# A planned attention-and-MLP kernel: first chunks loaded in parts, weight bits shifted in SBUF, two engines for low parts, another order of work

## The chip, the cores and the metric

The kernel runs on one core of a Trainium2 chip. The metric is the device time of an execution in microseconds (us), and three of them were taken. The engines are called PE (TensorE), PEld (its weight loads), DVE (VectorE), ACT (ScalarE), POOL (GpSimd) and SP (SyncE, which issues most loads here).

## What is computed

B is 4, H 8 heads of D = 64, S = 768 tokens, the model width 512. A decaying state per head gives y, and y goes through a gated layer: a causal convolution of five taps makes the gate, `w_val` and `w_out` are two 512x512 products.

```python
for t in range(S):
    state = gamma * state + einsum('bhd,bhe->bhde', k[:, :, t], v[:, :, t])
    y[:, :, t] = scale * einsum('bhd,bhde->bhe', q[:, :, t], state)
x = y.transpose(0, 2, 1, 3).reshape(B, S, H * D)
gate = 1 / (1 + exp(-causal_conv(x, conv_w)))     # 5 taps per channel
return (gate * (x @ w_val)) @ w_out
```

## The kernel before

The tokens are cut into 6 chunks of 128, times 4 batches: 24 groups, in the order chunk by chunk. `load` brings one group as a 1 MB tile `att` of four parts: q and k by dimension (parts 0 and 1), v and k by token (parts 2 and 3). Four such tiles exist (`LB`).

**Attention.** The four groups of chunk 0 go by `first_scores` (matmuls into the one score tile `sy`, L363), `first_mask` (DVE multiplies `sy` by a table, L396), `first_y` (matmuls into the one tile `ye`, L441) and `evac` (DVE copies `ye` times a decay into `x`, L504). `first_state` (L408) adds k times v to the state `z_ps`, after `decay` (POOL, L339) has scaled k. From group 4 on, `head` and then a `visit` and `rest_of_visit` per group do scores, state and y in one block of small matmuls (L424, L408, L424, L350), with `mask` (L372), `snap`, `turn` and `evac` on DVE and ACT.

**MLP.** Products run in three passes for accuracy: each operand is split into a high part (rounded by ACT) and a low part (value minus high part): `round_x` and `rest_x` for x (L514, L519), `round_gv` and `rest_gv` for the gated values (L632, L636), `cv_round` and `cv_low` for the weights (L577, L581). `val` (L610) makes a tile of 12 matmuls for each chunk and 128 channels, `outp` (L644) one for each chunk and batch: 48 tiles in all, called V and O below. `tap` (ACT L593 once, DVE L595 four times per tile) and `sigmoid` (ACT L602) make the gate, `gated` (DVE L625) multiplies it by the V tile in PSUM and so frees one of two banks `mm`. So a third V tile cannot start before `gated` has read the first.

**Weights.** The 8 weight tiles (w0 to w3 of `w_val`, w4 to w7 of `w_out`) arrive as 64-bit numbers in 512 KB pieces `wst`. Each is turned into fp32 by `cv_scale` (ACT, into a PSUM tile `acc`, L544), `cv_bits` (DVE shift and mask in `acc`, L548), `cv_top` (DVE, the sign from `wst`, the rest from `acc`, into `top`, L554), `cv_up` (ACT, L563) and `cv_sum` (POOL, L567); then `cv_round` on ACT and `cv_low` on POOL split it. The two `acc` tiles are those of the convolution.

**Order.** `plan` (L80 on) takes every step with a due time, an engine, a cost from the table `TIMES` and what it reads and writes, and writes out one order for all engines; a step with `other` may go to a second engine (no step has one before). `WORK` is the string of what PE does: s, y, z, p (first scores, y, state, table), h (head), v (visit), w (load a weight), V, O. `LOADS` is the order of the first loads on SP's queue. Where the plan sees PE idle at the start, it puts `filler` matmuls into `ye` (L672).

Of the kernel before, what the change touches and what calls it, by code (L numbers as in the profile page):

```python
# [21 lines left out]
LB = 4  # L22
# [230 lines left out]
def tile_retention_gated_mlp(  # L253
# [50 lines left out]
    masks = [  # L304
        mlp.tile([P, 512], F32, name="o_sb")[:, 0:384].rearrange("p (j k t) -> p j k t", j=2, t=HALF)
        for x in range(2)
    ]
# [71 lines left out]
    def first_table(x, part):  # L379


        vd = vd_sb[:, 0, 4 * x:4 * x + 4].rearrange("p (j s) -> p j s", s=2)
        if part == 0:
            nc.vector.tensor_tensor(
                masks[x][:, :, 0:3:2],
                vd.unsqueeze(3).broadcast_to([P, 2, 2, HALF]),
                tri_sb.unsqueeze(1).unsqueeze(1).broadcast_to([P, 2, 2, HALF]),
                op=ALU.mult,
            )
        else:  # L390
            nc.scalar.copy(masks[x][:, :, 1], vd[:, :, 0].unsqueeze(2).broadcast_to([P, 2, HALF]))

    def first_mask(g, x):
        if x == 0:
            us[g] = mlp.tile([P, 768], F32, name="u", bufs=2).rearrange("p (x j k t) -> p x j k t", x=2, j=2, t=HALF)
        nc.vector.tensor_tensor(  # L396
            us[g][:, x],
            sy[:, x, 0:384].rearrange("p (j k t) -> p j k t", j=2, t=HALF),
            masks[x],
            op=ALU.mult,  # L400
        )
# [133 lines left out]
    def cv_scale(n):  # L535


        size = high(n).shape[1]
# [5 lines left out]
        nc.scalar.mul(cvt[n][0].bitcast(F32), high(n).bitcast(F32), 2.0 ** -112)  # L544

    def cv_bits(n):
        bits = cvt[n][0]
        nc.vector.tensor_scalar(  # L548
            bits, bits, 3, 0x7FFFFFFF, op0=ALU.logical_shift_left, op1=ALU.bitwise_and
        )  # L550
# [25 lines left out]
    def cv_round(n):  # L576
        nc.scalar.copy(parts_of(n)[0], cvt[n][1].bitcast(F32))  # L577

    def cv_low(n):
# [1 line left out]
        nc.gpsimd.tensor_tensor(l, cvt[n][1].bitcast(F32), h.bitcast(F32), op=ALU.subtract)  # L581
# [282 lines left out]
    for p, (kind, n) in enumerate(LOADS):  # L864
# [3 lines left out]
        elif kind == "a":  # L868
            load_at(t, n)
        elif kind == "q":  # L870
            at(t, "DMA", 0.4, [], [("att", 0, "qk")], load, 0, slice(0, 2)).mb = 0.5
        elif kind == "v":
            at(t, "DMA", 0.4, [], [("att", 0, "vk"), ("att", 0, "kn")], load, 0, slice(2, 4)).mb = 0.5
# [142 lines left out]
```

## Time and profile before

| what | value |
|---|---|
| median of 3 runs | 214.03 us (213.93 to 215.69) |
| the profiled execution, its own time | 213.34 us |
| its span in the trace | 211.5 us |
| PE, DVE, ACT, POOL busy | 202.0, 125.3, 109.7, 106.0 us |
| granted PE clock | 0.999 |
| bytes read and written | 29.46 and 6.29 MB |

Busy time of PE also counts the fillers and the overlap of pipelined matmuls. A row of a timeline reads: start, length, engine, line, operation, tile written <- tiles read, shape, count, and in brackets the idle time before it with what ended it. In the trace each fp32 matmul of the attention is two records, so a block of 16 in the code is x32.

### The profile page before, as it was taken

Reading aid. Unit: us, or ns where it says so; the run is one execution under the profiler, and the core shown is the slowest. Engines: PE = TensorE matmul, PEld = TensorE weight load, DVE = VectorE, ACT = ScalarE, POOL = GpSimd, SP = SyncE. Lnnn points to the kernel's source line nnn. Section 1 sums busy time; section 2 is a strip of 40 time slices with the busy share of each in tenths; the row PEclk is TensorE's granted clock in tenths of the full one; section 3 lists DMA queues with packets and bytes.
Section 4 is the critical chain, followed back from the end, with each engine's and each line's share of the span. In section 5 each row is a group of like instructions: output and inputs, shape, how many; then the busy total and the mean of one; then the engine's idle time right before and its main releaser. Section 6 shows DMA issues by size and latency. Waiting matters only on the chain.

```text
span 211.5 us, 7837 instructions
## 1 busy us (share of the span) xinstructions
PE 202.0 (96%) x3500; PEld 160.1 (76%) x3500; DVE 125.3 (59%) x193; ACT 109.7 (52%) x237; POOL 106.0 (50%) x93
## 2 busy tenths in 40 slices
PE   8976799999999999999999999999999999999993
PEld 3655578876787887888888887877777788888883
DVE  0467799994889322799589813499505599211000
ACT  2377657974793533964686334455345445311321
POOL 0279987899953773538565336242044624202200
PEclk9999999999999999999999999999999999999999
DMA  6999995647656703866352715521110010121122
GB/s 196 395 418 412 417 373 198 228 181 229 270 203 198 277 29 110 293 234 268 124 225 108 262 38 206 181 116 50 53 53 3 3 50 0 51 100 51 50 101 99
DMA packets 8677, 36.24 MB, mean 171 GB/s; under 512 B 1090, under 2 KB 1474, under 8 KB 5700
## 3 DMA queue, kind: packets, MB, share of 16 engines
q1 hardware_dynamic: 4896, 29.43, 37.5%
q10 hardware_dynamic: 3748, 6.32, 7.9%
q8 instruction: 27, 0.44, 0.9%
q14 instruction: 6, 0.05, 0.1%
HBM read 29.46 MB, written 6.29 MB: 169 GB/s over the span
## 4 chain that ended last, share of the span: by engine, by line
PE 79%; POOL 6%; ACT 2%; DVE 2%; issue 1%; DMA 1%; ACTq 0%; DVEq 0%
PE mm L610 31%; PE mm L644 29%; PE sy L424 9%; PE sy L350 4%; PE z_ps L408 3%; POOL wol L581 2%; POOL top L567 2%; POOL gvl L636 1%; PE ye L672 1%; DMA out_dram<-o_sb 1%; DVE u L396 1%; DVE x L504 1%; PE ye L441 0%; ACT o_sb L654 0%; PE sy L363 0%
## 5 line engine op out<-in xcount | busy, mean ns | idle before, releaser
L595 DVE SCALAR_TENSOR_TENSOR acc<-x,cw_sb,acc 128x512 f32<-128x512 f32 x96 | 68.1, 752 | 4.6 <-ACT acc L593 3.4
L636 POOL TENSOR_TENSOR gvl<-gate,gvh 128x512 fp32r<-128x512 f32 x24 | 30.9, 1288 | 45.0 <-ACT gvh L632 42.2
L519 POOL TENSOR_TENSOR xl<-x,xh 128x512 fp32r<-128x512 f32 x24 | 30.8, 1286 | 31.2 <-ACT xh L514 29.6
L644 PE MATMUL mm<-wol,gvh 128*128 128x512 f32 (+1 forms) x100 | 37.8, 390 | 0.5 <-POOL wol L581 0.5
L644 PE MATMUL mm<-woh,gvh 128*128 128x512 f32 (+1 forms) x100 | 37.6, 390 | 0.0
L644 PE MATMUL mm<-woh,gvl 128*128 128x512 f32 (+1 forms) x100 | 37.5, 389 | 0.0
L610 PE MATMUL mm<-xh,wvh 128*128 128x512 f32 x96 | 35.3, 399 | 0.0
L610 PE MATMUL mm<-xl,wvh 128*128 128x512 f32 x96 | 33.9, 406 | 0.0
L339 POOL TENSOR_TENSOR att<-att,small_sb 128x512 f32<-128x512 f32 x24 | 25.1, 1048 | 12.0 <-DMA small_sb<-in_small_dram 6.8
L372 DVE TENSOR_TENSOR u<-sy,small_sb 128x512 f32<-128x512 f32 x20 | 13.8, 688 | 24.9 <-PE sy L350 20.8
L625 DVE TENSOR_TENSOR gate<-mm,gate 128x512 f32<-128x512 f32 x24 | 16.4, 685 | 20.0 <-PE mm L610 20.0
L610 PE MATMUL mm<-xh,wvl 128*128 128x512 f32 x96 | 26.6, 397 | 0.0
L654 ACT COPY o_sb<-mm 128x512 f32<-128x512 f32 (+1 forms) x25 | 14.3, 571 | 23.0 <-PE mm L644 22.1
L632 ACT CAST gvh<-gate 128x512 fp32r<-128x512 f32 x24 | 14.8, 617 | 18.8 <-DVE gate L625 18.0
L644 PEld LDWEIGHTS mm<-wol,gvh 128*128 128x128 f32 x100 | 18.7, 188 | 5.3 <-POOL wol L581 1.4
L644 PEld LDWEIGHTS mm<-woh,gvh 128*128 128x128 f32 x100 | 18.7, 188 | 4.5 <-ACT woh L577 0.3
L644 PEld LDWEIGHTS mm<-woh,gvl 128*128 128x128 f32 x100 | 18.7, 188 | 4.1
L602 ACT ACTIVATE gate<-acc 128x512 f32<-128x512 f32 x24 | 14.4, 602 | 14.2 <-DVE acc L595 8.4
L610 PEld LDWEIGHTS mm<-xh,wvh 128*128 128x128 f32 x96 | 17.8, 188 | 4.4 <-ACT xh L514 0.2
L610 PEld LDWEIGHTS mm<-xh,wvl 128*128 128x128 f32 x96 | 17.9, 188 | 4.2
L610 PEld LDWEIGHTS mm<-xl,wvh 128*128 128x128 f32 x96 | 17.7, 188 | 4.4
L514 ACT CAST xh<-x 128x512 fp32r<-128x512 f32 x24 | 14.9, 620 | 9.5 <-DVE x L504 9.3
(49 smaller groups left out, 249.4 us busy)
## 6 DMA issues: line engine op xcount, KB each, us to landing
att<-in_att_dram SPq DMA_DIRECT2D x23, 1024.0 KB, 5.1
out_dram<-o_sb ACTq DMA_DIRECT2D x23, 256.0 KB, 2.1
wst<-in_w_dram SPq DMA_DIRECT2D x8, 512.0 KB, 10.2
att<-in_att_dram SPq DMA_DIRECT2D x2, 512.0 KB, 4.5
out_dram<-o_sb ACTq DMA_DIRECT2D x2, 128.0 KB, 1.7
small_sb<-in_small_dram SPq DMA_DIRECT2D x1, 68.0 KB, 5.4
cw_raw<-in_conv_w_dram ACTq DMA_DIRECT2D x1, 20.0 KB, 5.3
u<-in_pos_dram ACTq DMA_DIRECT2D x1, 5.0 KB
```

What stands on the lines that cost most here:

```text
L339: nc.gpsimd.tensor_tensor(v, v, vd_sb[:, c, :].unsqueeze(2).broadcast_to([P, 8, HALF]), op=ALU.mult)
L424: nc.tensor.matmul(sy[cols, h, off:off + HALF], lhsT=lhsT, rhs=rhs, start=start, stop=True, skip_group_check=True,)
L514: nc.scalar.copy(xh[n][:, :, b], xs[n][:, :, b, HALO:])
L519: nc.gpsimd.tensor_tensor(xl[n][:, :, b], xs[n][:, :, b, HALO:], xh[n][:, :, b].bitcast(F32), op=ALU.subtract)
L595: nc.vector.scalar_tensor_tensor(acc, x[:, :, k:k + P], cw_sb[:, m, k:k + 1], acc, op0=ALU.mult, op1=ALU.add,)
L602: nc.scalar.activation(gate[n, m], accs.pop((n, m)), AF.Sigmoid)
L610: nc.tensor.matmul(vps[n, m], lhsT=w[:, m, ct * P:(ct + 1) * P], rhs=xx[n][:, ct].rearrange("p b t -> p (b t)"), start=(i == 0), stop=(i = ...
L625: nc.vector.tensor_tensor(gv, vps.pop((n, m)), gv, op=ALU.mult)
L632: nc.scalar.copy(gvs[n, m][0], gate[n, m])
L636: engine.tensor_tensor(gvl, gate.pop((n, m)), gvh.bitcast(F32), op=ALU.subtract)
L644: nc.tensor.matmul(ops[n, b, cs.start][:, 0:cs.stop - cs.start], lhsT=gg[:, b * P:(b + 1) * P], rhs=w[:, ct, cs], start=(i == 0), stop=(i ...
L654: nc.scalar.copy(o_sb[:, 0:step], ops.pop((n, b, cs.start))[:, 0:step])
```

## The change

The four first groups are loaded in parts: q and k by dimension first, then v, and k by token (part 3) as a piece of its own; of groups 1 to 3 that part comes after later weights. `first_mask` becomes one instruction for both halves of `sy`, and its table lies in a buffer of `xh` and no longer in two of `o_sb`. `cv_scale` writes into `top` in SBUF, and `cv_bits` and `cv_top` work there; PSUM's `acc` is left to the convolution. `cv_low` of all weights and `rest_x` of chunk 0 may be planned on POOL or on DVE. `WORK` and `LOADS` are other strings: six weights, not four, are in the first loads.

```diff
+    "bits": (0.43, 0.34),
...
-    def first_mask(g, x):
-        if x == 0:
-            us[g] = mlp.tile([P, 768], F32, name="u", bufs=2).rearrange("p (x j k t) -> p x j k t", x=2, j=2, t=HALF)
+    def first_mask(g):
+        us[g] = mlp.tile([P, 768], F32, name="u", bufs=2).rearrange("p (x j k t) -> p x j k t", x=2, j=2, t=HALF)
         nc.vector.tensor_tensor(
-            us[g][:, x],
-            sy[:, x, 0:384].rearrange("p (j k t) -> p j k t", j=2, t=HALF),
-            masks[x],
+            us[g].rearrange("p x j k t -> p x (j k t)"),
+            sy[:, :, 0:384],
+            masks.rearrange("p x j k t -> p x (j k t)"),
...
-    def rest_x(n, b):
+    def rest_x(n, b, engine=nc.gpsimd):
...
+    def rest_x_too(n, b):
+        rest_x(n, b, nc.vector)
...
         cvt[n] = (
-            ps_a.tile([P, 512], I32, name="acc")[:, 0:size],
             stage.tile([P, size], I32, name="top"),
...
     def cv_bits(n):
-        bits = cvt[n][0]
+        top = cvt[n][0]
         nc.vector.tensor_scalar(
-            bits, bits, 3, 0x7FFFFFFF, op0=ALU.logical_shift_left, op1=ALU.bitwise_and
+            top, top, 3, 0x7FFFFFFF, op0=ALU.logical_shift_left, op1=ALU.bitwise_and
         )
 
     def cv_top(n):
-        bits, top, _ = cvt[n]
+        top = cvt[n][0]
         nc.vector.scalar_tensor_tensor(
-            top, high(n), -0x80000000, bits, op0=ALU.bitwise_and, op1=ALU.bitwise_or
+            top, high(n), -0x80000000, top, op0=ALU.bitwise_and, op1=ALU.bitwise_or
         )
...
+    def cv_low_too(n):
+        cv_low(n, nc.vector)
...
-    LOADS = (("v", 0), ("q", 0), ("t", 0), ("w", 0), ("a", 1), ("a", 2), ("w", 1), ("a", 3), ("w", 2), ("w", 3))
+    LOADS = (("q", 0), ("t", 0), ("v", 0), ("k", 0), ("w", 0), ("a", 1), ("a", 2), ("w", 1), ("a", 3), ("w", 2), ("k", 1), ("w", 3), ("w", 4), ("k", 2), ("k", 3), ("w", 5))
...
-        "spysyssyyVwzzwzhzVVvwwvVvOvOOvOVvvVVVOvvOVv"
-        "vVVvVvOOvOVVvOVvOVOOVvOVvvVvOVVVOOOVOVOOOOO"
+        "spyzsyszysywVzzhVwvvVVOOvvOVvVvVVOOvvOVvvV"
+        "OOvVVvVvVOOVvvVOvOOvvVVvOOVvVOOOVOVVOVOOOO"
...
+        steps[-1].other = ("DVE", TIMES["DVE"], cv_low_too)
...
+        if n == 0:
+            steps[-1].other = ("DVE", TIMES["DVE"], rest_x_too)
```

How the planned order moves shows in three places (that of the loads stands in `LOADS`). The first is PE where the first V tile begins, behind the last `first_y` (L441 before, L440 in the change); L408 and L407 are `first_state` (x16) and the state half of the head (x8), L350 the head's scores, L610 and L614 the matmuls of V. Before:

```order
L441 MATMUL ye<-u,att 64x64 x8
L672 MATMUL ye<-const-float32-0.0 128x256 x2
L350 MATMUL sy<-att 64x64 x16
L408 MATMUL z_ps<-att 64x64 x8
L610 MATMUL mm<-xh,wvh 128x512 x4
```

Of the change:

```order
L440 MATMUL ye<-u,att 64x64 x8
L676 MATMUL ye<-const-float32-0.0 128x256
L407 MATMUL z_ps<-att 64x64 x16
L614 MATMUL mm<-xh,wvh 128x512 x4
L614 MATMUL mm<-xh,wvl 128x512 x4
L614 MATMUL mm<-xl,wvh 128x512 x2
L407 MATMUL z_ps<-att 64x64 x16
L614 MATMUL mm<-xl,wvh 128x512
L407 MATMUL z_ps<-att 64x64 x16
L614 MATMUL mm<-xl,wvh 128x512
L614 MATMUL mm<-xh,wvh 128x512 x2
L350 MATMUL sy<-att 64x64 x16
```

V begins ahead of two `first_state` and the head, which now lie between its matmuls; before, one `first_state` did (further down).

The second is DVE from the last `evac` of chunk 0 on (L504, in the change L503). Before:

```order
L504 TENSOR_TENSOR x<-ye,base 128x4x128
L548 TENSOR_SCALAR acc<-acc 128x512
L554 SCALAR_TENSOR_TENSOR top<-wst,acc 128x512
L595 SCALAR_TENSOR_TENSOR acc<-x,cw_sb,acc 128x512 x7
L372 TENSOR_TENSOR u<-sy,small_sb 128x2x256
```

Of the change:

```order
L503 TENSOR_TENSOR x<-ye,base 128x4x128
L582 TENSOR_TENSOR wvl<-top,wvh 128x512
L518 TENSOR_TENSOR xl<-x,xh 128x4x128
L599 SCALAR_TENSOR_TENSOR acc<-x,cw_sb,acc 128x512
L549 TENSOR_SCALAR top<-top 128x512
L599 SCALAR_TENSOR_TENSOR acc<-x,cw_sb,acc 128x512
L555 SCALAR_TENSOR_TENSOR top<-wst,top 128x512
L599 SCALAR_TENSOR_TENSOR acc<-x,cw_sb,acc 128x512 x3
L549 TENSOR_SCALAR top<-top 128x512
```

Two low parts that were POOL's stand in DVE's queue, and each conversion reads and writes `top`.

The third is where the last two weights, w6 and w7, get their low parts `wol`. Before, on POOL (L567 is `cv_sum`, L636 the low part of a gated tile, L519 that of x):

```order
L567 TENSOR_TENSOR top<-top,up 128x512
L339 TENSOR_TENSOR att<-att,small_sb 128x512
L567 TENSOR_TENSOR top<-top,up 128x512
L581 TENSOR_TENSOR wol<-top,woh 128x512
L636 TENSOR_TENSOR gvl<-gate,gvh 128x512
L581 TENSOR_TENSOR wol<-top,woh 128x512
L519 TENSOR_TENSOR xl<-x,xh 128x4x128
```

Of the change, on DVE (L555 is `cv_top`, L629 `gated`, L503 `evac`):

```order
L549 TENSOR_SCALAR top<-top 128x512
L555 SCALAR_TENSOR_TENSOR top<-wst,top 128x512
L372 TENSOR_TENSOR u<-sy,small_sb 128x2x256
L582 TENSOR_TENSOR wol<-top,woh 128x512
L629 TENSOR_TENSOR gate<-mm,gate 128x512
L503 TENSOR_TENSOR x<-sy,dec 128x4x128
L582 TENSOR_TENSOR wol<-top,woh 128x512
```

The last low part of the weights has gone from POOL's queue to DVE's, behind the fourth `gated`. In the whole program DVE takes two `rest_x` and three `cv_low` (w1, w6, w7), POOL keeps the others.

More of the change, by code (lines that the diff above doesn't have):

```diff
@@ L301, in tile_retention_gated_mlp @@
     ye = ps_m[0].tile([P, 2, 512], F32, name="ye")
[L304 to L307, printed above, removed]
+    masks = mlp.tile([P, NPAIR, B, P], F32R, name="xh", bufs=XS).bitcast(F32)[:, 0:2].rearrange(
+        "p a b t -> p (a b t)"
+    )[:, 0:768].rearrange("p (x j k t) -> p x j k t", x=2, j=2, t=HALF)
     steps = []
@@ L698, in load_at, with load_part_at @@
         at(due, "DMA", 0.4, [], [("att", g % LB, k) for k in ("qk", "vk", "kn")], load, g).mb = 1.0
-    first_u = {}
+    def load_part_at(due, g, first, last):
+        keys = [("att", g % LB, k) for k, part in (("qk", 0), ("vk", 2), ("kn", 3)) if first <= part < last]
+        at(due, "DMA", 0.4, [], keys, load, g, slice(first, last)).mb = 0.25 * (last - first)
+    first_u, mask_slot = {}, Slot("xh", XS)
     def first_scores_at(t, g):
@@ L707, in first_scores_at @@
         steps[-1].wide = 1.5
-        for x in range(2):
-            masked = [("mask", x, 0), ("mask", x, 1), sc]
-            at(t + 0.02 + 0.01 * x, "DVE", (0.555, 0.475), masked + [first_u[g]] * x, [first_u[g], ("fu", g, x)][x:], first_mask, g, x)
+        at(t + 0.02, "DVE", (0.955, 0.875), [mask_slot, sc] + [("mask", x, k) for x in range(2) for k in range(2)], [first_u[g]], first_mask, g)
     def first_y_at(t, g):
         y, vk = Slot("ye", 1), ("att", g % LB, "vk")
-        at(t, "PE", 0.5, [first_u[g], ("fu", g, 0), ("fu", g, 1), vk], [y, "early"], first_y, g).small = 32
+        at(t, "PE", 0.5, [first_u[g], vk], [y, "early"], first_y, g).small = 32
         steps[-1].wide = 1.5
@@ L778, in convert @@
         raw = wsts[n] if n != "cw" else "cwraw"
-        acc, top, up = Slot("acc", 2), Slot("top", 2), Slot("up", 2)
+        top, up = Slot("top", 2), Slot("up", 2)
         k = 0.3 if n == "cw" else 1.0
@@ L783, in cost @@
             return tuple(k * x for x in TIMES[e])
-        at(t, "ACT", cost("ACT"), [raw], [acc, top, up], cv_scale, n)
-        at(t + 0.01, "DVE", cost("DVE"), [], [acc], cv_bits, n)
+        at(t, "ACT", cost("ACT"), [raw], [top, up], cv_scale, n)
+        at(t + 0.01, "DVE", cost("bits"), [], [top], cv_bits, n)
         at(t + 0.02, "ACT", cost("ACT"), [raw], [up], cv_up, n)
-        at(t + 0.03, "DVE", cost("DVE"), [raw, acc], [top], cv_top, n)
+        at(t + 0.03, "DVE", cost("DVE"), [raw], [top], cv_top, n)
         at(t + 0.04, "POOL", cost("POOL"), [up], [top] if n != "cw" else [top, "cw"], cv_sum, n)
@@ L867, in tile_retention_gated_mlp @@
             at(t, "DMA", 0.4, [], ["small"], get, small_sb, small, nc.sync).mb = 0.2
[L868 to L873, printed above, removed]
+        elif kind in "aqvk":
+            load_part_at(t, n, *{"a": (0, 3), "q": (0, 2), "v": (2, 3), "k": (3, 4)}[kind])
         else:
@@ L876, in tile_retention_gated_mlp @@
     for x in range(2):
-        at(0.3 + 0.01 * x, "DVE", (0.42, 0.35), ["small"], [("mask", x, 0)], first_table, x, 0)
-        at(0.32 + 0.01 * x, "ACT", (0.25, 0.2), ["small"], [("mask", x, 1)], first_table, x, 1)
+        for k, (engine, cost) in enumerate((("DVE", (0.42, 0.35)), ("ACT", (0.25, 0.2)))):
+            first = x == k == 0
+            at(
+                5.0 + 0.01 * x + 0.02 * k, engine, cost, ["small"] + [mask_slot] * (not first),
+                [mask_slot] * first + [("mask", x, k)], first_table, x, k,
+            )
     early = [n for kind, n in LOADS if kind == "w"]
```

18 lines of the change are left out of this document (9 added, 9 removed).

## The prediction

> **What bounds the kernel now.** I read the page, then the busy times by stretch, the chain that ended last, the groups by line, and the timeline up to 62 us. The busy times by stretch first; the columns are the stretch, then busy us and instructions of PE, PEld, DVE, ACT and POOL, the granted clock, the DMA share and GB/s.
>
> ```profile
> 7.00:26.44 19.44, 15.12 (x418) 11.20 (x417) 14.20 (x25) 13.67 (x31) 15.82 (x15) 1.00 1.02 419
> 26.44:36.00 9.56, 9.56 (x139) 7.48 (x142) 9.49 (x15) 5.79 (x14) 7.91 (x7) 1.00 0.84 316
> 36.00:53.00 17.00, 16.48 (x485) 12.94 (x480) 13.41 (x22) 12.71 (x30) 15.99 (x14) 1.00 0.60 201
> 62.00:80.00 18.00, 18.00 (x318) 14.46 (x318) 10.07 (x15) 8.08 (x18) 11.66 (x10) 1.00 0.48 169
> ```
>
> There are three stages. Up to 26.4 us loads fill the DMA engines (share 1.02, 419 GB/s) while PE partly runs fillers. Up to 53 us the weights are converted: DVE is full first (9.49 of 9.56 us), then POOL (15.99 of 17). After that PE has no gap to speak of. So the end is set by when PE gets real work and how long it waits for converted weights; what remains then runs at PE's pace. The chain (start, us, what) shows the hand-over:
>
> ```profile
> 51.51 1.29 POOL wol L581
> 52.84 4.23 PE mm L644 x17
> ...
> 63.10 1.15 PE mm L610 x5
> 64.25 0.62 PE sy L424 x32
> 64.88 0.47 PE z_ps L408 x32
> 65.34 0.50 PE sy L424 x31
> 65.85 0.47 PE sy L350 x32
> 66.31 2.30 PE mm L610 x9
> ...
> 205.67 0.59 ACT o_sb L654
> ```
>
> At 52.84 PE takes the low part of the last weight, w7, right behind POOL. From there to 205.67 the chain stays on PE but for short waits.
>
> PE's prices: 30 matmuls of a tile take 7.00 us, 0.233 each. A visit takes 64.25 to 66.31, and the nine matmuls behind it 0.20 more than 9 x 0.233: 2.26. A `first_state` between V matmuls is 0.62 plus 0.21 (18 x 0.233 is 4.19, not 4.40): 0.83. A head is 0.62 + 0.23 + 0.20 = 1.05.
>
> ```profile
> 169.61 7.00 PE mm L610 x30
> ```
> ```profile
> 25.58 0.62 PE sy L350 x32
> 26.20 0.23 PE z_ps L408 x16
> 26.44 0.66 PE mm L610 x2
> 29.89 0.62 PE z_ps L408 x32
> 30.52 4.40 PE mm L610 x18
> ```
>
> **Part 1: the earlier start.** The first landing that the trace shows as a wait is that of group 1:
>
> ```profile
> 10.91 1.04 POOL L339 TENSOR_TENSOR att<-att,small_sb 128x512 f32<-128x512 f32 x1 [2.49 <-DMA att<-in_att_dram]
> 12.07 0.90 PE L363 MATMUL sy<-att 64*64 64x128 f32 x32
> 17.64 1.01 DVE L396 TENSOR_TENSOR u<-sy,o_sb 128x384 f32<-128x384 f32 x2
> 9.62 0.95 PE L441 MATMUL ye<-u,att 64*64 64x128 f32 x32
> 23.70 0.69 DVE L504 TENSOR_TENSOR x<-ye,base 128x512 f32<-128x512 f32 x1 [1.21 <-PE ye L441]
> 25.05 0.60 ACT L514 CAST xh<-x 128x512 fp32r<-128x512 f32 x1
> 26.37 1.20 PE L610 MATMUL mm<-xh,wvh 128*128 128x512 f32 x4
> ```
>
> Ahead of it lay 2.57 MB with its own, now 2.32: 0.25 MB at 419 GB/s is 0.6 us, so 10.3. Groups 2 and 3 come 0.5 and 0.75 MB earlier (before, by the same rate, 13.3 and 16.9; now 12.1 and 15.1). The single `sy` and `ye` make a chain: scores 0.95, mask 1.0 (the joined one saves about 0.05), y 0.95. So s1 10.3, mask 11.5 (behind w0's `cv_top`), y1 to 13.4, s2 to 14.35, mask to 15.3, then on DVE w1's shift and top and `evac`, mask 3 to 18.2, y3 to 19.2. Behind mask 3 stand w2's shift and top, the last `evac` ends near 20, its xh near 20.7: V starts there and not at 26.37. A slower load is hidden in this chain by up to 0.6 us. The pieces moved back (part 3 of groups 1 to 3 and their `decay`) are wanted by the `first_state` inside the first V tile; 5.07 MB are in by 17, and POOL has them done when PE gets there. SP issues two DMAs more, 0.33 us each, ahead of need.
>
> Two edits are free: `cv_scale` writes SBUF instead of PSUM on ACT, which is busy 5.79 of 9.56 us in the next stage and would hide a tenth of a us each; and the mask's table lies in a buffer of xh that chunk 1 wants only after its first `evac`, behind the fourth mask. Without that cover each would add its own length, under 0.7, once per weight or once.
>
> The order puts one more `first_state` and the head into the V stream: +1.88 us of PE.
>
> **Part 2: the weights.** Counting the order up to the first matmul that reads w7's low part: before 66 tile matmuls, one `first_state` and 4 visits; in the change 65, two, the head, and 2 visits. So behind that point the change has 0.23 + 2 x 2.26 = 4.75 us more to do. The end is unchanged if w7's low part comes at 52.84 - 4.75 = 48.1, and moves with it. PE alone could be there at 20.7 + 65 x 0.233 + 2 x 0.83 + 1.05 + 2 x 2.26 = 43.1.
>
> That part is now the last of a long row on DVE, which works in order and serves `gated`, too (PE's banks). Its prices, one start to the next:
>
> ```profile
> 24.30 0.69 DVE L548 TENSOR_SCALAR acc<-acc 128x512 int32<-128x512 int32 x1
> 30.43 0.68 DVE L372 TENSOR_TENSOR u<-sy,small_sb 128x512 f32<-128x512 f32 x1
> 31.03 0.68 DVE L625 TENSOR_TENSOR gate<-mm,gate 128x512 f32<-128x512 f32 x1
> 31.63 2.86 DVE L595 SCALAR_TENSOR_TENSOR acc<-x,cw_sb,acc 128x512 f32<-128x512 f32 x4
> ```
>
> 0.60 per instruction, 0.70 per tap (the first three of 2.86 after 0.75 for the last). From mask 3 to w7's low part the order has 16 taps (11.2), and 26 others: 6 shifts, 6 tops, 4 `gated`, 3 masks, 3 `evac`, 4 low parts (15.6): 26.8. With 0.6 for waiting on the scores of visits: 18.2 + 26.8 + 0.6 = 45.6. The shift is taken at the price it has from PSUM, its nearest row; what it costs in SBUF no row shows. At worst it is that, at best its 512 elements go at double rate: 20 elements take 0.18, so 0.51 becomes 0.26, six times 0.25 = 1.5 less (44.1).
>
> ```profile
> 11.30 0.18 DVE L548 TENSOR_SCALAR acc<-acc 128x20 int32<-128x20 int32 x1
> ```
>
> **Part 3: two engines at SBUF.** Before, only L384 on DVE reads two SBUF tensors, twice, and it ran beside POOL. In these rows times are ns min/median/max:
>
> ```profile
> L384 DVE TENSOR_TENSOR o_sb<-small_sb x2: 424/844/1265, 7.1 to 7.4; 128x256 f32<-128x256 f32 x2
> L595 DVE SCALAR_TENSOR_TENSOR acc<-x,cw_sb,acc x96: 745/751/757, 25.7 to 180.3; 128x512 f32<-128x512 f32 x96
> ```
> ```profile
> 7.21 1.21 POOL L339 TENSOR_TENSOR att<-att,small_sb 128x512 f32<-128x512 f32 x1 [6.77 <-DMA small_sb<-in_small_dram]
> 8.63 1.01 DVE L396 TENSOR_TENSOR u<-sy,o_sb 128x384 f32<-128x384 f32 x2
> ```
>
> The first took 0.42; the second, begun while POOL worked from 7.21 to 8.42, took 1.27 and ended about 0.3 behind POOL; POOL's own took 1.21, not 1.04. The taps, with one input in SBUF and one in PSUM, ran beside POOL 96 times within 2% of each other. So two SBUF inputs on DVE wait for POOL, and POOL for them. In the change `cv_top` has two (`wst`, `top`; before, PSUM was one), and so have the low parts on DVE: from mask 3 on 6 tops and 4 low parts, ten. What does one wait? Nothing at the least; a whole POOL instruction's rest, 0.62 on average for one of 1.25, at the most. POOL is busy 15.82 of 19.44, which gives 0.50; of six tops some three meet a POOL that waits for that top. I take 0.35, 3.5 in all: w7 at 49.1, 1.0 behind 48.1.
>
> ```profile
> 49.04 1.28 POOL L581 TENSOR_TENSOR wol<-top,woh 128x512 fp32r<-128x512 f32 x1
> 50.27 1.28 POOL L636 TENSOR_TENSOR gvl<-gate,gvh 128x512 fp32r<-128x512 f32 x1
> ```
>
> POOL gives away five instructions of 1.25, 6.2 us, which is what makes the early start possible, and gets back up to 0.5 for each of DVE's ten.
>
> The Trainium skill (SBUF — State Buffer, Who interferes with whom) says the same of two SBUF inputs, and adds that a `tensor_scalar` in a two-port mode also shuts GpSimd out, the later one waiting until the other is done. VectorE: DVE Perf Modes (The perf-mode tier table) gives fp32 `tensor_scalar` out of SBUF twice the rate. By these pages the shift gains 1.5 and waits six times 0.35: w7 at 49.7, 0.6 later than by the rows. No run here shows it.
>
> The sum: +1.0. The profiled execution took 213.34 (span 211.5, 1.8 around it), so 214.3 on its scale; the median of the runs is 0.69 above it, so **215.0**. With the shift at its best and all else the same 213.5; with waits of 0.50 216.5. That is the likeliest case's own range.
>
> **Rivals.**
> *The engines don't hinder each other*, because most instructions find POOL between two others. For it: POOL has 3.6 us free up to 26.4, and only one pair of rows speaks against. Then w7 comes at 45.6 or 44.1, 2.5 or 4.0 before 48.1: 210.0 to 211.5; I say 210.5.
> *Everything on DVE that converts waits a full rest*, the shifts too. It stands at w2's shift, right behind mask 3, where POOL has `rest_x` to do, and goes on to w7. 16 x 0.62 = 9.9 on 44.1 gives 54.0: 220; at 0.50 each 52.1, 218. `gated` then frees PE's banks late, too. It decides from a mean wait of 0.25 on. I say 218. Against it: waiting makes POOL idle, too.
> *The loads don't come earlier*, since the pieces queue on SP behind landings. Then mask 3 ends as before at 21.9, 3.7 later, and w7 with it: 218.7. Against it: SP issues far ahead while the DMA engines are full.
>
> ```profile
> 21.34 0.55 DVE L396 TENSOR_TENSOR u<-sy,o_sb 128x384 f32<-128x384 f32 x1
> ```
>
> **How the numbers follow.** A run of this kernel can tell about 1% from no change. The forecast gets 0.39 (of which faster 0.05, same 0.22, slower 0.12), no hindrance 0.33 (faster 0.31, same 0.02), full waits 0.23 (same 0.03, slower 0.20), late loads 0.05 (same 0.03, slower 0.02). That makes faster 0.36, same 0.30, slower 0.34. The range reaches from just below 210 to 218, since the two outer cases hold more than half: 209.6 to 218.0.
>
> **What would show it.** The first V matmul near 21 to 23 us, not 26.4. L555, L582 and L518 on DVE spread between 0.68 and 1.3 as L384 did, the taps still at 0.75; if L555 stays at 0.68 throughout, there is no hindrance. L549: 0.69 or 0.44. A wait of PE for DVE's `wol` near 49; POOL no longer in that place. I am wrong if DVE is through with w7 before 46 or behind 51, if V starts behind 25, or if PE behind 62 us shows gaps that it did not have.

## The result and the profile after

| | before | changed |
|---|---|---|
| median of 4 runs | 213.98 us | 221.12 us (219.43 to 221.90) |
| ratio, with its 95% interval | | 1.030 (1.022 to 1.039): slower |
| profiled execution, its own time | 213.34 us | 221.77 us |
| its span; granted PE clock | 211.5 us; 0.999 | 220.0 us; 0.969 |

The kernel before has one run more here than ahead of the prediction. The forecast was 215.0 with a range up to 218.0. The sign of its middle value was right, but that was hardly a call (its chances were 0.36 for faster and 0.34 for slower), and the size was far too small. The steps of the prediction are on the profiled executions, where the loss is 8.4 us.

The busy times by stretch of the changed kernel come first (stretch, then busy us and instructions of PE, PEld, DVE, ACT and POOL, granted clock, DMA share, GB/s), the last stretch of the kernel before behind them:

```profile
7.00:26.40 19.40, 14.00 (x301) 10.30 (x301) 15.82 (x19) 12.20 (x27) 12.04 (x11) 0.83 0.98 386
26.40:36.00 9.60, 9.60 (x136) 7.16 (x136) 9.07 (x15) 5.80 (x13) 7.02 (x6) 0.82 0.83 301
36.00:48.00 12.00, 10.57 (x283) 8.54 (x282) 12.00 (x17) 8.36 (x17) 11.37 (x10) 1.00 0.49 167
48.00:62.00 14.00, 11.36 (x203) 8.08 (x205) 8.39 (x10) 6.11 (x14) 9.97 (x8) 0.88 0.29 109
62.00:200.00 138.00, 137.60 (x2464) 111.58 (x2454) 86.60 (x131) 71.19 (x156) 59.91 (x50) 1.00 0.39 141
```
```profile
62.00:200.00 138.00, 137.54 (x2257) 111.33 (x2256) 80.26 (x120) 65.70 (x142) 59.18 (x49) 1.00 0.34 123
```

Behind 62 us PE is as full as it was. The loss lies before: PE idles 1.43 us in 36 to 48 and 2.64 in 48 to 62 (before the change 0.32 and 0.20), the granted clock is below 1 in three stretches, and DVE, which has taken over work of POOL, is busy 12.00 of 12 (11.49 before). PE's timeline shows whom it waits for (start, us, idle before and what ended it):

```profile
23.74 1.22 PE L676 MATMUL ye<-const-float32-0.0 128*128 128x256 f32 x2 [2.61 <-DVE x L503]
25.95 2.07 PE L614 MATMUL mm<-xh,wvh 128*128 128x512 f32 x4
52.64 0.50 PE L648 MATMUL mm<-wol,gvh 128*128 128x512 f32 x1 [2.18 <-DVE wol L582]
56.39 0.99 PE L648 MATMUL mm<-wol,gvh 128*128 128x512 f32 x2
```

V's first matmul is at 25.95, hardly ahead of the 26.37 of before. The first product with w7's low part starts at 56.39 and not at 52.84. In DVE's groups (ns min/median/max) the reason stands:

```profile
L549 DVE TENSOR_SCALAR top<-top x9: 177/789/1433, 9.7 to 48.1; 128x512 int32<-128x512 int32 x8, 128x20 int32<-128x20 int32 x1
L555 DVE SCALAR_TENSOR_TENSOR top<-wst,top x8: 678/1019/1656, 12.2 to 48.9; 128x512 int32<-128x512 int32 x8
L582 DVE TENSOR_TENSOR wol<-top,woh x2: 1351/1404/1458, 51.1 to 54.4; 128x512 fp32r<-128x512 f32 x2
L518 DVE TENSOR_TENSOR xl<-x,xh x2: 981/1254/1526, 13.9 to 25.0; 128x512 fp32r<-128x512 f32 x2
L599 DVE SCALAR_TENSOR_TENSOR acc<-x,cw_sb,acc x96: 741/749/757, 26.4 to 190.3; 128x512 f32<-128x512 f32 x96
```

The shift and the combining step (`cv_top`, which now reads two SBUF tensors) spread over a microsecond, and no low part (two SBUF tensors as well) comes below 0.98 us; the taps, with one input in PSUM, stay within 2%. What an instruction waits for is seen when DVE's timeline is laid beside POOL's. DVE:

```profile
16.55 1.43 DVE L549 TENSOR_SCALAR top<-top 128x512 int32<-128x512 int32 x1
48.94 1.66 DVE L555 SCALAR_TENSOR_TENSOR top<-wst,top 128x512 int32<-128x512 int32 x1
51.12 1.46 DVE L582 TENSOR_TENSOR wol<-top,woh 128x512 fp32r<-128x512 f32 x1
54.39 1.35 DVE L582 TENSOR_TENSOR wol<-top,woh 128x512 fp32r<-128x512 f32 x1 [0.61 <-ACT woh L578]
```

POOL at the same times:

```profile
16.42 1.27 POOL L518 TENSOR_TENSOR xl<-x,xh 128x512 fp32r<-128x512 f32 x1
48.59 1.46 POOL L640 TENSOR_TENSOR gvl<-gate,gvh 128x512 fp32r<-128x512 f32 x1
50.77 1.26 POOL L568 TENSOR_TENSOR top<-top,up 128x512 int32<-128x512 int32 x1 [0.72 <-DVE top L555]
53.91 1.28 POOL L640 TENSOR_TENSOR gvl<-gate,gvh 128x512 fp32r<-128x512 f32 x1 [0.18 <-ACT gvh L636]
```

POOL's ends are 17.69, 50.05, 52.03 and 55.19; DVE's are 17.98, 50.60, 52.58 and 55.74. The shift ends 0.29 behind POOL, the other kinds 0.55: DVE's instruction gets through only when POOL's has ended, and then takes nearly its own time. Of the sixteen such instructions behind mask 3, fifteen end 0.27 to 0.56 behind a POOL instruction; the one left, the combining step at 32.39, meets POOL idle and takes 0.68.

### The profile page after: what moved, and what is told of

Read it like the earlier page. It is cut to its first block, busy times and chain, and to the rows that moved or that the text cites. A ratio compares the mean times of both kernels' runs of the same rounds, so it can differ in the third digit from the quotient of the medians.

```text
span 220.0 us, 7826 instructions
## 1 busy us (share of the span) xinstructions
PE 206.0 (94%) x3492; PEld 162.1 (74%) x3492; DVE 134.1 (61%) x194; ACT 110.6 (50%) x237; POOL 103.5 (47%) x88
## 4 chain that ended last, share of the span: by engine, by line
PE 83%; DVE 11%; issue 2%; ACT 1%; DMA 1%; DVEq 0%; ACTq 0%
PE mm L648 30%; PE mm L614 29%; PE sy L423 10%; PE z_ps L407 5%; PE sy L350 4%; DVE acc L599 3%; DVE top L555 3%; PE ye L670 2%; DVE top L549 2%; PE ye L676 1%; PE sy L363 1%; PE ye L440 1%; DMA out_dram<-o_sb 1%; DVE x L503 1%; DVE u L372 1%
## 5 line engine op out<-in xcount | busy, mean ns | idle before, releaser
L599 DVE SCALAR_TENSOR_TENSOR acc<-x,cw_sb,acc 128x512 f32<-128x512 f32 x96 | 67.0, 750 | 4.3 <-ACT acc L597 3.9
L518 POOL TENSOR_TENSOR xl<-x,xh 128x512 fp32r<-128x512 f32 x22 | 28.8, 1310 | 46.6 <-ACT xh L513 46.6
L640 POOL TENSOR_TENSOR gvl<-gate,gvh 128x512 fp32r<-128x512 f32 x24 | 31.6, 1315 | 34.7 <-ACT gvh L636 34.6
L648 PE MATMUL mm<-woh,gvh 128*128 128x512 f32 (+1 forms) x100 | 38.2, 397 | 0.9 <-DVE gate L629 0.5
L648 PE MATMUL mm<-woh,gvl 128*128 128x512 f32 (+1 forms) x100 | 38.3, 398 | 0.0
L614 PE MATMUL mm<-xl,wvh 128*128 128x512 f32 x96 | 34.0, 407 | 0.0
L339 POOL TENSOR_TENSOR att<-att,small_sb 128x512 f32<-128x512 f32 x24 | 27.4, 1142 | 13.2 <-DMA att<-in_att_dram 10.8
L614 PE MATMUL mm<-xh,wvh 128*128 128x512 f32 x96 | 33.3, 411 | 0.0
L629 DVE TENSOR_TENSOR gate<-mm,gate 128x512 f32<-128x512 f32 x24 | 16.4, 685 | 19.3 <-PE mm L614 19.3
L614 PE MATMUL mm<-xh,wvl 128*128 128x512 f32 x96 | 27.7, 408 | 0.0
L636 ACT CAST gvh<-gate 128x512 fp32r<-128x512 f32 x24 | 14.9, 620 | 23.0 <-DVE gate L629 22.9
L648 PEld LDWEIGHTS mm<-woh,gvh 128*128 128x128 f32 x100 | 19.2, 192 | 6.3 <-DVE gate L629 0.9
L503 DVE TENSOR_TENSOR x<-sy,dec 128x512 f32<-128x512 f32 x20 | 13.7, 683 | 15.4 <-PE sy L423 8.3
L614 PEld LDWEIGHTS mm<-xh,wvh 128*128 128x128 f32 x96 | 18.2, 193 | 4.7 <-ACT o_sb L658 0.2
L614 PEld LDWEIGHTS mm<-xh,wvl 128*128 128x128 f32 x96 | 18.3, 194 | 4.4
L614 PEld LDWEIGHTS mm<-xl,wvh 128*128 128x128 f32 x96 | 18.1, 191 | 4.5
```

The lines of the kernel that those rows point to most:

```text
L339: nc.gpsimd.tensor_tensor(v, v, vd_sb[:, c, :].unsqueeze(2).broadcast_to([P, 8, HALF]), op=ALU.mult)
L503: nc.vector.tensor_tensor(xs[c][:, :, b, HALO:].rearrange("p (h j) t -> p h j t", h=2), y.rearrange("p h (j t) -> p h j t", t=P), decs[c]. ...
L518: engine.tensor_tensor(xl[n][:, :, b], xs[n][:, :, b, HALO:], xh[n][:, :, b].bitcast(F32), op=ALU.subtract)
L599: nc.vector.scalar_tensor_tensor(acc, x[:, :, k:k + P], cw_sb[:, m, k:k + 1], acc, op0=ALU.mult, op1=ALU.add,)
L614: nc.tensor.matmul(vps[n, m], lhsT=w[:, m, ct * P:(ct + 1) * P], rhs=xx[n][:, ct].rearrange("p b t -> p (b t)"), start=(i == 0), stop=(i = ...
L629: nc.vector.tensor_tensor(gv, vps.pop((n, m)), gv, op=ALU.mult)
```

## Experiments

Three theories were named in the expectations. A: VectorE and GpSimd hinder each other at SBUF, and that is the loss. B: the order of the work or of the loads is to blame. C: the clock that TensorE loses by idling is. Each run is compared with runs of the kernel before on the same chip (213.4 to 213.6).

### e1_shift_in_sbuf: the order of before, only the bits in SBUF

```diff
+        top = stage.tile([P, size], I32, name="top")
         cvt[n] = (
-            ps_a.tile([P, 512], I32, name="acc")[:, 0:size],
-            stage.tile([P, size], I32, name="top"),
+            top, top,
             stage.tile([P, size], I32, name="up"),
         )
```

> The kernel before with its own order kept row for row; only the weights' bits lie in SBUF (scale, shift and top all work on the tile top). Theory A (VectorE and GpSimd hinder each other at SBUF): L548 and L554, which took 0.69 and 0.68 us, now spread from 0.43 and 0.68 to about 1.5, some 16 instructions with 0.5 us of waiting each; the kernel before had 2 us of slack at most of PE's waits, so 215.5 to 219 us. Theory B (the searched order is to blame, not the place of the bits): the same order costs the same, 213 to 214.5 us.

218.09 us, ratio 1.022 (1.020 to 1.024): 4.6 more, with no instruction moved, and inside what A expected. The groups of this run, and POOL's last low part in its timeline:

```profile
L548 DVE TENSOR_SCALAR top<-top x9: 416/706/1227, 11.5 to 49.3; 128x512 int32<-128x512 int32 x8, 128x20 int32<-128x20 int32 x1
L554 DVE SCALAR_TENSOR_TENSOR top<-wst,top x8: 687/1159/1648, 13.8 to 50.2; 128x512 int32<-128x512 int32 x8
```
```profile
55.97 1.27 POOL L581 TENSOR_TENSOR wol<-top,woh 128x512 fp32r<-128x512 f32 x1
```

Before, the two groups stood at 690 and 680 ns nearly throughout. w7's low part ends at 57.24 instead of 52.79, 4.45 later; the profiled time is 217.80, 4.46 more than before. So the bits in SBUF cost 4.6 us by themselves, without any new order: the shift there, which the change makes for its double rate, together with the combining step, whose second input has moved to SBUF with it.

### e2_pool_reads_less: the changed order, most of POOL's reads taken away

```diff
     def cv_sum(n):
         top, up = cvt[n]
+        if n != "cw":
+            return nc.gpsimd.memset(up, 0)
...
     def cv_low(n, engine=nc.gpsimd):
         h, l = parts_of(n)
+        if engine is nc.gpsimd: return engine.memset(l.bitcast(F32), 0.0)
```

POOL's low parts of the first x likewise. This kernel so leaves out the sums of the weights and the low parts that POOL makes.

> The changed kernel with its own order kept; GpSimd's low parts of the weights and of the first chunk's x, and the sums of the weights, are replaced by memsets of the same tiles, so that GpSimd reads nothing in SBUF there (the low halves of the weights and most low parts are left out of the result). The decays and the low parts of the gated tiles stay. Theory A: VectorE's shift takes 0.43 and its top 0.68 nearly everywhere, the low part of the last weight is done before 46 us instead of 55.7, and the time is 208 to 211 us, 3 to 6 below the kernel before. Theory B: VectorE's queue stays as long as it is, and the time stays above 217 us. Theory C (the cold clock of PE is the cost): PE would still idle before its first V tile, 216 us or more.

215.45 us, ratio 1.009 (1.006 to 1.013): 1.9 us over the kernel before, where the changed kernel is 7.1 over it. So 5.2 us of the loss go with these reads, in the changed order. The number of theory A, 208 to 211, is missed all the same. Some of POOL's reads were left (decays, the low part of the gated values), and V starts at 22.80, 3.2 earlier than in the changed kernel, but not at 20.7. POOL's own work is shorter too with writes of 0.52 us, and the rounding of a weight no longer waits for POOL's sum, so a part of the gain may be that; but the last low parts of w are DVE's, in this run as in the changed kernel. Three views of this run, DVE's groups, DVE's timeline and POOL's:

```profile
L549 DVE TENSOR_SCALAR top<-top x9: 177/419/1085, 9.7 to 43.2; 128x512 int32<-128x512 int32 x8, 128x20 int32<-128x20 int32 x1
L555 DVE SCALAR_TENSOR_TENSOR top<-wst,top x8: 674/686/1672, 12.6 to 43.6; 128x512 int32<-128x512 int32 x8
```
```profile
29.17 0.70 DVE L549 TENSOR_SCALAR top<-top 128x512 int32<-128x512 int32 x1
35.81 0.67 DVE L555 SCALAR_TENSOR_TENSOR top<-wst,top 128x512 int32<-128x512 int32 x1
43.61 1.67 DVE L555 SCALAR_TENSOR_TENSOR top<-wst,top 128x512 int32<-128x512 int32 x1
```
```profile
29.07 0.53 POOL L582 MEMSET wol<- 128x512 f32 x1
35.57 0.53 POOL L569 MEMSET up<- 128x512 int32 x1 [1.21 <-ACT up L564]
43.31 1.42 POOL L640 TENSOR_TENSOR gvl<-gate,gvh 128x512 fp32r<-128x512 f32 x1 [2.54 <-ACT gvh L636]
```

At 35.81 the combining step runs beside a POOL instruction that only writes, and takes its 0.67; at 43.61 it meets one that reads and takes 1.67, up to 0.55 behind POOL's end at 44.73. The shift differs: at 29.17 it waits even for an instruction that only writes and ends 0.27 behind it, at 29.87.

### e3_shift_strided: the shift in every second word

```diff
             stage.tile([P, size], I32, name="up"),
+            stage.tile([P, size, 2], I32, name="bits" if n != "cw" else "bits_cw", bufs=1)[:, :, 0])
```

> The changed kernel with its own order; only the shift works in a tile of every second word, so that it should go at one element per cycle, 0.68 us, with one input in SBUF. Theory A in the form of the prediction (only two SBUF inputs hinder): it never hindered anyone, 0.25 us more for each of 8, 222 to 224 us. Theory A with the rule that a shift at double rate also takes the way that GpSimd uses: all shifts take 0.68 to 0.70 without spread, their 2.6 us of waiting go and 2 us come, and GpSimd is held up less: 219 to 221 us. If the shift spreads up to 1.4 us all the same, any VectorE instruction in SBUF is held up.

221.25 us, ratio 1.037 (1.034 to 1.040): as the changed kernel.

```profile
L548 DVE TENSOR_SCALAR bits<-bits x8: 429/808/1440, 10.4 to 48.3; 128x512 int32<-128x512 int32 x8
```

The group of its shifts shows nearly the same least, middle and longest time as in the changed kernel (0.43, 0.79 and 1.43). A distance of 8 bytes between the words takes away neither the rate nor the waits, so the run tells nothing about whether they hang together.

### e4_loads_only and e7_loads_only_z0_behind_y0: the loads alone

On the kernel before, with the first chunks in parts and their keys later; everything else as before, but the order is planned anew. In the second run one step is moved in the finished plan:

```diff
+        z0 = next(x for x in order if x.fn is first_state and x.args == (0,))
+        order.remove(z0)
+        y0 = next(x for x in order if x.fn is first_y and x.args == (0,))
+        order.insert(order.index(y0) + 1, z0)
```

> The kernel before with the first chunks loaded in parts (keys by token later), planned again with its own string of work; bits in PSUM, low parts by GpSimd, two masks as before. Theory A: the loads themselves help; the first V matmul comes 2 to 3 us earlier (23 to 24.5 us), GpSimd's conversions then decide, and 212 to 213.5 us results. Theory B: replanning with these loads already costs, 215 us or more.

> The kernel of the run with the loads alone (first chunks without their keys, bits in PSUM, low parts by GpSimd, two masks; it took 217.36), with z0 moved behind the first y of group 0 and nothing else. Theory B (late keys in front of y0): GpSimd idles 3.4 us before its first low part of x there and VectorE 4.7 us before evac 0; both come 1.5 us earlier and GpSimd is full behind them, so 215.5 to 216.5. If the order of the rest is to blame instead: within 0.7 of 217.4.

217.36 us, ratio 1.020 (1.016 to 1.024), and 216.20, ratio 1.010 (1.006 to 1.014). The loads do not pay by themselves; 1.2 of their 3.9 us come from the first state, which stands ahead of the first y on PE and needs keys that land late. PE's and POOL's timelines of the first of the two:

```profile
9.70 0.69 PE L408 MATMUL z_ps<-att 64*64 64x64 f32 x32 [1.51 <-POOL att L339]
```
```profile
8.60 1.04 POOL L339 TENSOR_TENSOR att<-att,small_sb 128x512 f32<-128x512 f32 x1 [8.16 <-DMA att<-in_att_dram]
13.06 1.27 POOL L519 TENSOR_TENSOR xl<-x,xh 128x512 fp32r<-128x512 f32 x1 [3.42 <-ACT xh L514]
```

PE stands 1.51 us for the decayed keys with y0 queued behind, and POOL then stands 3.42 us for what follows from y0.

### e5_z0_behind_y0: the same step moved in the changed kernel

> The changed kernel with one step moved: the first state's 32 small matmuls of group 0 (z0), which need the keys of group 0 by token, stand on TensorE behind the first y of group 0 instead of ahead of it; every other instruction is where it was. Theory A (VectorE and GpSimd hinder each other): VectorE is full from 20 us on, so only what reaches it earlier counts; evac 0 comes 1.4 to 1.7 us earlier (from 11.6 to about 10.0), about half of it survives the chain, 219.5 to 221. Theory B (the loads with z0 ahead of y0 cost by themselves, through the late keys): the delay of group 0 is the cause of what hindrance does not explain, and all of it comes back: 218.5 to 219.5. Theory C (TensorE's clock falls when it idles): without the idle 1.5 us at 8 us the clock stays at 1.00 in 8 to 13 us.

The edit is the one above. 221.65 us, ratio 1.034 (1.027 to 1.040): nothing gained. DVE's timeline:

```profile
10.89 0.68 DVE L503 TENSOR_TENSOR x<-ye,base 128x512 f32<-128x512 f32 x1
13.09 0.96 DVE L395 TENSOR_TENSOR u<-sy,xh 128x768 f32<-128x768 f32 x1 [0.91 <-PE sy L363]
```

The first `evac` comes 0.7 earlier than in the changed kernel (11.62), but group 1's mask at 13.09, as there (13.02): it waits for scores that are not earlier. These stand behind y0 and z0 both, whichever of the two goes first, on a PE at a granted clock of 0.50 in 10 to 13 us. A and B expected a gain here, and both were wrong: the late keys cost the changed order nothing. C's expectation failed too: the granted clock is 0.89 in 7 to 22 us, as without the edit.

### e6_shift_in_psum: the changed kernel with its bits in PSUM

```diff
+        bits = ps_a.tile([P, 512], I32, name="acc")[:, 0:size]
...
-        top, up = Slot("top", 2), Slot("up", 2)
+        acc, top, up = Slot("acc", 2), Slot("top", 2), Slot("up", 2)
```

> The changed kernel with the weights' bits back in a PSUM bank (scale writes it, shift works in it, the combining step reads one operand from it); the loads, the one mask and the low parts on either engine stay as in the changed kernel. The order of the steps is worked out anew under the PSUM bank's limits. Theory A: the six shifts and six combinations between 20 and 56 us lose their waits (2.6 + 3.2 = 5.8 us) and the shift goes from 0.43 back to 0.69 (6 x 0.26 = 1.6 us more): 4.3 us off the time of w7's low part, 216.5 to 218. Theory B (loads and order to blame): no less than 219.5.

218.48 us, ratio 1.018 (1.010 to 1.026): 2.6 less than the changed kernel and half a us above the 216.5 to 218 of A; the interval reaches into that of the changed kernel (1.022 to 1.039). DVE's groups, then rows of DVE and of ACT:

```profile
L551 DVE TENSOR_SCALAR acc<-acc x9: 187/690/700, 8.5 to 47.7; 128x512 int32<-128x512 int32 x8, 128x20 int32<-128x20 int32 x1
L557 DVE SCALAR_TENSOR_TENSOR top<-wst,acc x8: 673/678/689, 11.8 to 48.9; 128x512 int32<-128x512 int32 x8
```
```profile
30.98 0.70 DVE L551 TENSOR_SCALAR acc<-acc 128x512 int32<-128x512 int32 x1 [2.87 <-ACT acc L547]
36.06 0.75 DVE L601 SCALAR_TENSOR_TENSOR acc<-x,cw_sb,acc 128x512 f32<-128x512 f32 x1
28.95 0.62 ACT L580 CAST wvh<-top 128x512 fp32r<-128x512 f32 x1 [2.83 <-POOL top L570]
```

The waits of the shift and of the combining step are gone to the last. Other waits stand in their place. DVE idles 2.87 us for ACT's scale, which is queued behind a rounding that waits 2.83 us for POOL's sum. And the first tap stands at 36.06 instead of 26.43, in a plan in which bits and convolution share the two PSUM banks again. How much of the rest of the loss each makes is not shown.

### e8_low_by_pool: all low parts on POOL

```diff
-        steps[-1].other = ("DVE", TIMES["DVE"], cv_low_too)
...
-        if n == 0:
-            steps[-1].other = ("DVE", TIMES["DVE"], rest_x_too)
```

> The changed kernel with all low parts on GpSimd, as in the kernel before; the shift stays in SBUF, loads and mask as changed, order worked out anew. Theory A: VectorE gives up five instructions of 1.2 to 1.4 us before w7 (7 us), GpSimd takes 5 x 1.04 to 1.3 us more where it was 15.7 us of 17 busy, so GpSimd becomes the bound and w7's low part comes 0 to 3 us earlier or later: 219 to 224. A rival, that moving the low parts to VectorE was the mistake and the shift harmless: 215 to 217.

225.13 us, ratio 1.051 (1.045 to 1.058), a us beyond what A expected, and the rival (215 to 217) is out. At w7's low part PE now waits for POOL, as A expected; its longest waits up to 62 us, 2.28 and 2.12, are for an `evac` on DVE:

```profile
56.90 0.50 PE L648 MATMUL mm<-wol,gvh 128*128 128x512 f32 x1 [1.06 <-POOL wol L582]
```

### e9_keep_warm: matmuls of zeros in two gaps

```diff
+            nc.tensor.matmul(
+                bank, lhsT=warm.broadcast_to([P, P]), rhs=warm.broadcast_to([P, 512]),
+                start=False, stop=False, skip_group_check=True,
+            )
```

> The changed kernel with matmuls of zeros added in two gaps in which TensorE waits for VectorE: eleven behind the last first y (21 to 23.7 us; they add zeros to the state's bank) and nine ahead of the first product with weight tile 6's low part (50.4 to 52.6 us; they add zeros to the open output bank). Nothing else moves. Theory C (the clock falls when TensorE idles): the granted clock stays at 1.00 in 24 to 28 and in 54 to 56; of this only the second counts, because the first tiles wait for VectorE anyway: the nine products between 52.64 and 56.39 are done by 55, so the first product with tile 7's low part goes at 55.8 instead of 56.4 and the next ones at full speed, 0.6 to 1.2 us less, 220.5 to 221.2. If the clock does not follow from idling: clock and time unchanged, or a little slower.

220.26 us, ratio 1.030 (1.026 to 1.034). The granted clock does what C said; windows of the changed kernel, then of this one:

```profile
24.00:28.00 4.00, 4.00 (x39) 2.84 (x40) 4.00 (x5) 3.44 (x7) 4.00 (x4) 0.50 0.58 206
54.00:56.00 2.00, 2.00 (x7) 1.51 (x6) 1.35 (x1) 0.88 (x2) 2.00 (x2) 0.50 0.00 0
```
```profile
24.00:28.00 4.00, 4.00 (x76) 2.90 (x69) 4.00 (x6) 2.55 (x7) 4.00 (x4) 1.00 0.92 358
54.00:56.00 2.00, 2.00 (x86) 1.64 (x90) 0.00 (x0) 0.27 (x2) 2.00 (x2) 1.00 0.00 0
```

PE's timeline at w7's low part, which ends at 53.94 here:

```profile
53.99 0.73 PE L648 MATMUL mm<-wol,gvh 128*128 128x512 f32 x2 [0.44 <-DVE wol L582]
```

PE now stands ready for it and takes it at once, where the changed kernel came 0.65 us late. (That everything in this profiled execution is earlier is no effect of the edit alone: it is a us ahead at the first added matmul already, with a granted clock of 1.00 in 8 to 13 us where the changed kernel's has 0.66, and it is the fastest of its four.) The median is 0.9 less than the changed kernel's and a little below what was expected, but the ratio to the kernel before is the same. That matmuls in these gaps keep the clock up is shown; what the low clock costs is not settled.

### e10_before_low_either and e11_before_low_either_one_mask: the low parts, then the mask, on the kernel before

```diff
+        steps[-1].other = ("DVE", TIMES["DVE"], cv_low_too)
...
+        if n == 0:
+            steps[-1].other = ("DVE", TIMES["DVE"], rest_x_too)
```

> The kernel before with one part of the change alone: low parts of the weights and of the first x may go to VectorE (the planner puts seven of them there); bits stay in PSUM, loads, masks and the order's string stay as before. Theory A: each low part on VectorE beside a busy GpSimd takes 0.7 to 1.4 us; VectorE was 11.49 of 12 us busy in 36 to 48, so what GpSimd is relieved of is paid there: 213 to 216. If the hindrance of the low parts is small: GpSimd, which was full from 18 us, is relieved by seven times 1.27 us, the first V tile comes a microsecond earlier and no product waits for a low part: 211.5 to 213.

> As the run before, with the one first mask of the change too (one VectorE instruction of 0.95 us instead of two of 0.55): 0 to 0.5 us less than that run, since the mask stands between the scores and y of each first group.

218.28 us, ratio 1.021 (1.017 to 1.026), and 218.53, ratio 1.022 (1.018 to 1.026). DVE's groups in the first of the two:

```profile
L584 DVE TENSOR_TENSOR wol<-top,woh x4: 837/1034/1521, 44.5 to 55.9; 128x512 fp32r<-128x512 f32 x4
L584 DVE TENSOR_TENSOR wvl<-top,wvh x2: 1059/1274/1489, 21.0 to 30.9; 128x512 fp32r<-128x512 f32 x2
L519 DVE TENSOR_TENSOR xl<-x,xh x1: 1764/1764/1764, 18.8 to 18.8; 128x512 fp32r<-128x512 f32 x1
```

All seven wait, one of them a whole microsecond, and the loss is larger than A expected (213 to 216). The joined mask is worth nothing that can be measured.

### e12_planner_told: an order made for the measured prices

```diff
-    "bits": (0.43, 0.34),
+    "bits": (0.80, 0.72), "top": (1.05, 0.96), "low": (1.40, 1.31),
```

The last two stand where the planner took DVE's 0.69 for the combining step and a low part.

> The changed kernel with the planner told what the instructions took beside GpSimd: the shift 0.80 instead of 0.43, the combining step 1.05 and a low part on VectorE 1.40 instead of 0.69 each; same loads, same mask, same string. It moves one low part of w more back to GpSimd. Rival theory (the order was made for prices that do not hold, and an order for the right ones recovers the loss): 214 to 217. Theory A (the waits themselves are the loss, whoever stands where; 16 of 0.56 us before w7, of which only those of one or two low parts go, and GpSimd has little room): 218.5 to 222.

224.20 us, ratio 1.049 (1.046 to 1.053): the rival is out, and it was worse than A expected too. PE's timeline has the longest wait here, on DVE, again at the output products:

```profile
54.20 0.50 PE L648 MATMUL mm<-woh,gvh 128*128 128x512 f32 x1 [3.41 <-DVE gate L629]
```

## Why the prediction was wrong, point by point

**What bounds the kernel: right.** The end moves with w7's low part, and PE behind 62 us is as full as before.

**Part 2's break-even: right, and to half a us in five kernels.** All with the order of the change (in e5 but for one step); the forecast of the third column is 213.34 + (second - 48.1):

| kernel | first product with w7's low part | by the formula | profiled time |
|---|---|---|---|
| changed | 56.39 | 221.6 | 221.77 |
| e2 | 50.21 | 215.5 | 215.28 |
| e3 | 56.42 | 221.7 | 221.92 |
| e5 | 56.43 | 221.7 | 222.11 |
| e9 | 53.99 | 219.2 | 219.11 |

**Part 3, "I take 0.35, 3.5 in all": the step that failed.** From mask 3 to w7's low part sixteen instructions were exposed, not ten: the six shifts wait as well. Taking each one's time less its time without POOL (0.43 for the shift, 0.68 for the others), the shifts waited 2.6 us, the combining steps 3.2 and the low parts 3.1: 8.9, a mean of 0.56. So two things were wrong in this term: the ten that it counts waited 6.3 and not 3.5, 0.63 each, no less than the 0.62 that it had named as the most, and the six shifts that it put at nothing waited 2.6. The discount from 0.50 to 0.35, for tops that find POOL waiting for them, had no row behind it: POOL has decays and low parts of gated values to do in between. It was the rival "everything on DVE that converts waits a full rest" that happened, with 16 x 0.56 for its 16 x 0.50, and its condition (from a mean wait of 0.25 on) was met twice over; it got 0.23 where it deserved most. Its own 218 to 220 is short, too, since it starts from the same mask 3.

The rule that the prediction cited from the Trainium skill (SBUF — State Buffer, Who interferes with whom) carries this: two SBUF inputs on DVE, or a `tensor_scalar` at double rate, against GpSimd, the later one waiting until the other is done. The rows above agree, with 0.29 and 0.55 us left to do after POOL's end, and e2 agrees with its other half, that two inputs do not contend with an instruction that only writes (0.67 at 35.81), while the shift does (0.70 at 29.17). The prediction gave the rule its sentence and then left the shifts out of the sum because no row showed them.

**The shift's price: too high.** DVE's timeline has one that POOL did not meet:

```profile
10.28 0.43 DVE L549 TENSOR_SCALAR top<-top 128x512 int32<-128x512 int32 x1 [0.17 <-ACT top L545]
```

Taken at 0.60 from start to start, after PSUM's row of 0.69, it is about 0.35 here by the same overlap of 0.08: double rate, 1.5 less over six, the best case that the prediction had named. In e1 this saving came with 4.6 us of loss.

**Part 1, "V starts there and not at 26.37": wrong, 25.95 instead of 20.7.** Mask 3 ended at 20.17, not at 18.2, and the last `evac` at 23.68, not near 20. DVE's timeline holds the larger part of it:

```profile
20.57 1.07 DVE L549 TENSOR_SCALAR top<-top 128x512 int32<-128x512 int32 x1 [0.40 <-ACT top L545]
21.67 1.41 DVE L555 SCALAR_TENSOR_TENSOR top<-wst,top 128x512 int32<-128x512 int32 x1
```

These two, a shift and a combining step, stand ahead of the last `evac` and wait 0.64 and 0.73 us; the shift at 16.55 (shown further up), ahead of the third `evac` and of mask 3, waits 1.00. The prediction counted no waits ahead of mask 3, and none ahead of V. Another microsecond comes from group 1, whose scores began at 11.40 on PE and not at 10.3; e5 shows that moving z0 does not bring it back. The landing itself was put too early. In e9's profiled execution, where PE was free sooner, the same scores wait for it:

```profile
11.09 0.90 PE L363 MATMUL sy<-att 64*64 64x128 f32 x32 [0.87 <-DMA att<-in_att_dram]
```

Before, that group's landing ended a wait at 10.91, so a quarter of a megabyte less ahead of it made it no earlier. The DMA engines moved 269 GB/s on average in the first 10.3 us of the changed kernel, 292 before; why is open. (The `att` loads are 29 instead of 25, four more and not two.)

**The sum again, with what was measured.** Forecast: 49.1 for w7's low part. Mask 3 +2.0, waits +5.4 (8.9 instead of 3.5), DVE idle +0.9 (1.5 instead of 0.6), shift -1.5: 55.9; measured 55.74. PE comes to it at 56.39, 0.65 later, since it works at half clock from 54 to 56. That gives +8.3 where +1.0 stood. Two of the prediction's own signs of being wrong appeared: DVE through with w7 behind 51, and V behind 25.

**The other rivals.** "The loads don't come earlier" happened for group 1 (11.09 in e9, 10.91 before), not for the later groups: their scores start at 14.75 and 17.40 instead of 15.22 and 18.71, and mask 3 ends at 20.17, not at the 21.9 of this rival. "The engines don't hinder each other" is out by e1. B, which was formed after the result, found no support in the changed kernel: e5 gained nothing, an order for the measured prices lost (e12), and e2 won its 5.2 us with the order kept. That no other order would do better is not shown. B is true of the loads put into the old order, where e7 won back 1.2 us.

**What stays open.** e2 leaves 1.9 us over the kernel before. Reads that it left to POOL bear on it (at 43.61 a top waits 1.0), and so does the start; no run tells how much each makes. And the shift, the low parts and the loads each cost 2.6 to 4.8 us alone, more in sum than the change as a whole: of those runs all but e1 have an order of their own, and no run tells what of their loss is that order's. No version here beats the kernel before; what is left to try is a way for the shift to read PSUM without taking a convolution's bank.

## What to carry to other kernels

Before moving an operand from PSUM to SBUF for its rate, ask which engines share the way to SBUF: beside a POOL that is busy most of the time (7.02 of 9.60 us, then 11.37 of 12.00) each exposed DVE instruction waited on average nearly half a POOL instruction, 0.56 us of 1.27, which is more than a shift takes. A rule of that kind that bears on a step goes into the sum with the full count of instructions that it names, not at a discount. And a break-even found once (when must this part be there?) is worth more than the estimate fed into it: it held within 0.5 us over five kernels.

## What the runs showed of the hardware that was not expected

- The granted PE clock was 0.50 behind gaps of 2.6 and 2.2 us in which PE waited (in 24 to 28 and in 54 to 56); with matmuls of zeros in the gaps it stayed at 1.00. The Trainium skill (TensorE: Matmul & The Clock Gate, Part 1: The HAM clock gate) names an idle window of about 3.4 us for the same fall; here it came behind shorter gaps.
- The length of a gap does not decide this alone: the clock stayed at 1.00 behind a gap of 2.40 us in e10 (PE waits for DVE's mask until 21.10) and of 3.41 us in e12 (until 54.20). And it was 0.50 in 10 to 12 us of the changed kernel, where no wait of PE ahead was longer than 0.77.
- A shift of 512 int32 words that start 8 bytes apart takes 0.43 us on DVE, as without a gap, and waits for POOL as much.
- The waits go both ways: in e10 a low part on DVE took 1.76 us, 1.07 more than its own 0.69, and in the changed kernel POOL's instructions of 1.27 stretch to 1.74 where DVE was first.
- A shift in SBUF waits even for a POOL `memset`, which only writes; a combining step with two SBUF inputs does not (e2).
- A POOL `memset` of 512 words takes 0.52 us, under half of the 1.27 of an instruction with two inputs.
